# Two-layer MLP behind a retention: VectorE makes the low parts of the first MLP's weights, and the first block's queues stand in another order

## The chip, the cores and the metric

One core of a Trainium2 chip runs the whole program as one launch. The metric is the device time of that launch in microseconds, the median over several executions. TensorE multiplies, VectorE, ScalarE and GpSimd do the elementwise work, and SyncE issues every DMA. Each engine works through its own queue in the order in which the program was written (the kernel fixes its schedule by hand), and waits at the head of the queue until what the next instruction needs is there.

## The reference

The reference computes a retention over 4 sequences of 576 tokens with 8 heads of 64 dimensions, then two MLPs on the 2304 tokens of 512 features.

```
scores = q @ k.T / 8
ret    = scores * gamma_h ** (i - j)   for i >= j, else 0
x      = ret @ v                        # heads side by side: 2304 x 512
h  = relu(x @ w_in)                     # 512 -> 2048
x1 = (h * h) @ w_out                    # 2048 -> 512
h2  = x1 @ w2_in
out = (h2 * clip(h2 + 3, 0, 6) / 6) @ w2_out
```

All inputs and outputs are float32.

## The kernel before

Tokens come in chunks of 128, and blocks of chunks: the first MLP goes over blocks of 512, 384, 512, 384 and 512 tokens, then the second MLP over five blocks. The 2048 hidden features are 16 slices of 128, called `f`. One step is one slice in one block: `h_part` multiplies the block's `x` by slice `f` of the first weight and makes `g`, and `a_part` multiplies `g` by slice `f` of the second weight into accumulators that stay in PSUM for the whole block.

Float32 products are made of three passes in a narrower float format. Each operand is split into a high part (the value rounded to that format) and a low part (the value less its high part), and a product is high times high, plus low weight times high, plus high weight times low. So each of `h_part` and `a_part` is 12 matmuls of up to 512 columns: four pieces of 128 by three terms.

The weights arrive as 64-bit words and are taken apart in the first block, while the matmuls of that block already run. For slice `f`, half 0 is the first weight and half 1 the second:

- `load_w` issues the DMA for each half (512 KB each).
- `scale_w` (lines 128 and 129) is two ScalarE operations on the raw words.
- `narrow_w` (lines 144 and 145) is two VectorE operations that make the float32 value `wt`.
- `split_w` makes the high part `w[:, 0]` by a copy, on ScalarE (line 156), or for half 1 from slice 2 on VectorE (line 154, a cast), and the low part `w[:, 1]` by a subtraction (line 158): on GpSimd for the first MLP's weights, on VectorE for the second's, whose weights are taken apart in the same buffers while the last block of the first MLP runs.

For one step `h_part` ends with ScalarE's relu (line 459), VectorE's product `r` (460), ScalarE's copy of it to the high part of `g` (466, in the first block; in later blocks VectorE does it, 468) and VectorE's subtraction for the low part (469).

The retention of the first block's four chunks stands ahead of all this (`first_scores`, `first_values`, `first_x` and so on). `first_sum` makes the running state, four small VectorE operations for each chunk. The chunks of the next block, three of them for the second, are worked on between the steps of the block before, one piece in each step: `scale_k` and `age_state` on GpSimd, `scores` on TensorE with its followers on VectorE (`p` at line 366 or 370, state at 381 or 383) and `scale_q` on GpSimd, `values` on TensorE with `x` on ScalarE and VectorE (429, 430), and `load_chunk` for a chunk further on.

The loop at line 624 goes over all steps and writes, for step `f` of the first block, in this order: narrow half 1 of slice `f+1`, split half 0 of `f+2`, split half 1 of `f+1`; `h_part` of step `f+1`; the loads; the retention's piece; narrow half 0 of `f+3`; the scales of half 1 of `f+2` and half 0 of `f+4`; `a_part` of step `f`. Two accumulators' worth of PSUM for `h` and two buffers of `g` let TensorE run about one step ahead of VectorE's `g`.

Of the kernel before, what the change touches and what calls it, by code (L numbers as in the profile page):

```python
# [9 lines left out]
F32 = mybir.dt.float32  # L10
# [5 lines left out]
ALU = mybir.AluOpType  # L16
# [7 lines left out]
NC = DM // P  # L24
NF = DFF // P
# [56 lines left out]
def retention_moe_kernel(ctx: ExitStack, tc, qk, kv, w1, w2, cst, out):  # L82
# [5 lines left out]
    nc = tc.nc  # L88
# [24 lines left out]
    def load_w(ph, f, halves=(0, 1)):  # L113

        src = (w1, w2)[ph].bitcast(I32)
        for i in halves:
            t = wpool.tile([P, DM, 2], I32, tag=f"w{f}_{i}", name=f"raw_{ph}_{f}_{i}")
            nc.sync.dma_start(
                t, src[f, :, 2 * DM * i : 2 * DM * (i + 1)].rearrange("p (n t) -> p n t", t=2)
            )  # L120
            raws[ph, f, i] = t

    def scale_w(ph, f, halves=(0, 1)):
        for i in halves:
            raw = raws[ph, f, i]
            low, high = raw[:, :, 0], raw[:, :, 1]
            high = high.bitcast(F32)
            nc.scalar.activation(high, high, AF.Prelu, scale=2.0**-112, alpha=-(2.0**32))  # L128
            nc.scalar.activation(low, low.bitcast(U32), AF.Copy, scale=2.0**-29)  # L129
# [18 lines left out]
    def split_w(ph, f, halves=(0, 1), on_dve=False):  # L148

        for i in halves:  # L150
            t = wts[ph, f, i]
            w = wpool.tile([P, 2, DM], F32R, tag=f"w{f}_{i}", name=f"w_{ph}_{f}_{i}")
            if on_dve:
                nc.vector.tensor_copy(w[:, 0, :], t)
            else:
                nc.scalar.activation(w[:, 0, :], t, AF.Copy)  # L156
            eng = nc.vector if ph else nc.gpsimd
            eng.tensor_tensor(w[:, 1, :], t, w[:, 0, :].bitcast(F32), ALU.subtract)  # L158
            wts[ph, f, i] = w


# [8 lines left out]
    n0 = BLOCKS[0][0][0] // P  # L170
# [3 lines left out]
    def load_chunk(c):  # L174
        if c >= NCHUNK:
            return
        if 2 <= c < n0:
            t = wpool.tile([P, 2, NPAIR, P], F32, tag=f"w{NF - 2}_{c % 2}", name=f"q_{c}")
            kv_t = wpool.tile([P, 2, DM], F32, tag=f"w{NF - 3}_{c % 2}", name=f"kv_{c}")
        else:  # L180
            t = rawp.tile([P, 2, NPAIR, P], F32, tag="q", name=f"q_{c}")
            kv_t = rawp.tile([P, 2, DM], F32, tag="kv", name=f"kv_{c}")
        q, kt = t[:, 0], t[:, 1]
        if c == 0:
            nc.sync.dma_start(q, qk[c, :, 0, :].rearrange("p (n t) -> p n t", n=NPAIR))
            nc.sync.dma_start(con[:, QD0:DK0], cst[:, QD0:DK0])
            nc.sync.dma_start(kt, qk[c, :, 1, :].rearrange("p (n t) -> p n t", n=NPAIR))
            nc.sync.dma_start(con[:, :QD0], cst[:, :QD0])
            nc.sync.dma_start(kv_t[:, 1], kv[c, :, 1])
        else:  # L190
            nc.sync.dma_start(t, qk[c].rearrange("p x (n t) -> p x n t", n=NPAIR))
        if 2 <= c < n0:
            nc.sync.dma_start(kv_t, kv[c])
        elif c >= n0:

            for g in range(2):
                nc.sync.dma_start(
                    kv_t[64 * g : 64 * g + 64].rearrange("t x (r e) -> t x r e", r=2),
                    kv[c, :, :, 4 * D * g : 4 * D * (g + 1)].rearrange("(r t) x e -> t x r e", r=2),
                )  # L200
        ch[c] = q, kt, kv_t[:, 0, :], kv_t[:, 1, :]
        if c == 1:
            nc.sync.dma_start(ch[0][2], kv[0, :, 0])
            nc.sync.dma_start(kv_t, kv[1])
# [87 lines left out]
    def first_sum(c):  # L292
        st = sts.pop(c)
        for e in range(2):
            r = slice(64 * e, 64 * e + 64)
            s0, s = (state[i % 2][r, :, 64 * e : 64 * e + 64] for i in (c, c + 1))
            g = gc[r].unsqueeze(2).to_broadcast([64, NPAIR, 64])
            if c == 0:
                nc.vector.tensor_tensor(s, st[r], g, ALU.mult)
            else:  # L300
                nc.vector.tensor_tensor(s, st[r], s0, ALU.add)
                nc.vector.tensor_tensor(s, s, g, ALU.mult)
# [135 lines left out]
    def h_part(ph, blk, f):  # L438
        nb = BLOCKS[ph][blk][0]
        w = wts[ph, f, 0]  # L440
        x = xs[ph, blk]
        hp = ps_h.tile([P, 512], F32, tag="h", name=f"h_{ph}_{blk}_{f}")
        order = [(c, wi, xi) for wi, xi in ((0, 0), (1, 0), (0, 1)) for c in range(NC)]

        parts = 2 if ph == blk == f == 0 else 1
        for i in range(parts):
            ts = slice(i * nb // parts, (i + 1) * nb // parts)
            for k, (c, wi, xi) in enumerate(order):
                nc.tensor.matmul(  # L449
                    hp[:, ts],  # L450
                    w[:, wi, c * P : (c + 1) * P],
                    x[:, xi, c, ts],
                    start=k == 0,
                    stop=k == 3 * NC - 1,
                )
        r = tmpp.tile([P, 512], F32, tag="tmp", name=f"r_{ph}_{blk}_{f}")
        r = r[:, :nb]
        if ph == 0:
            nc.scalar.activation(r, hp[:, :nb], AF.Relu)  # L459
            nc.vector.tensor_tensor(r, r, hp[:, :nb], ALU.mult)  # L460
        else:
            nc.scalar.activation(r, hp[:, :nb], AF.Relu, bias=con3)  # L462
            nc.vector.scalar_tensor_tensor(r, r, 6.0, hp[:, :nb], ALU.min, ALU.mult)  # L463
        g = gpool.tile([P, 2, 512], F32R, tag="g", name=f"g_{ph}_{blk}_{f}")
        if ph == 0 and blk == 0:
            nc.scalar.activation(g[:, 0, :nb], r, AF.Copy)  # L466
        else:
            nc.vector.tensor_copy(g[:, 0, :nb], r)  # L468
        nc.vector.tensor_tensor(g[:, 1, :nb], r, g[:, 0, :nb].bitcast(F32), ALU.subtract)  # L469
        gts[ph, blk, f] = g  # L470
# [138 lines left out]
    split_w(0, 0, (1,))  # L609
    first_states(3)  # L610
    h_part(0, 0, 0)
    scale_w(0, 1, (1,))
    load_chunk(n0)
    load_chunk(n0 + 1)
    narrow_w(0, 2, (0,))
    split_w(0, 2, (0,))

# [6 lines left out]
    for i, (ph, blk, f) in enumerate(steps):  # L624
        if ph == 0 and blk == 0 and f + 1 < NF:
            narrow_w(0, f + 1, (1,))
            if 2 < f + 2 < NF:
                split_w(0, f + 2, (0,))
            split_w(0, f + 1, (1,), on_dve=f > 0)
            if f == 0:  # L630
                first_sum(n0 - 1)
        if i + 1 < len(steps):
            h_part(*steps[i + 1])
        if ph == 0:
            if blk == 0:
                if f + 4 < NF:
                    load_w(0, f + 4)
            if blk + 1 < nblk:
                n = BLOCKS[0][blk + 1][0] // P

                j, slot = divmod(f - 1, 5) if blk == 0 else divmod(f, 4)
                if f == 0:
                    new_x(0, blk + 1)
                if 0 <= j < n:
                    c = start[0][blk + 1] // P + j
                    if slot == 0:
                        scale_k(c)
                        age_state(c)
                    elif slot == 1:
                        scores(c)  # L650
                        scale_q(c)
                    elif slot == (3 if blk == 0 else 2):
                        values(c, xs[0, blk + 1], j * P)
                    elif slot == (4 if blk == 0 else 3):
                        load_chunk(c + 2)
            elif f == 0:
                attn_stack.close()
                pool2 = ctx.enter_context(tc.tile_pool(name="pool2", bufs=1))
        if ph == 0 and blk == 0:
            if f == 0:  # L660
                scale_w(0, 3, (0,))
            if f + 3 < NF:
                narrow_w(0, f + 3, (0,))
            for n, j in ((f + 2, 1), (f + 4, 0)):
                if n < NF:
                    scale_w(0, n, (j,))
        for stage, fn in enumerate((split_w, narrow_w, scale_w)):
            for n in todo.get(i - (nblk - 1) * NF + stage, ()):
                fn(1, n // 2, (n % 2,))
        a_part(ph, blk, f)  # L670
        if ph == 0 and blk == nblk - 1:
            load_w(1, f)
            if 8 <= f < 8 + NC:
                load_x1(0, f - 8)
        if ph == 1 and blk + 1 < nblk and 8 <= f < 8 + NC:
            load_x1(blk + 1, f - 8)
# [37 lines left out]
```

## Time and profile before

| | us |
|---|---|
| median of 3 runs | 875.55 |
| lowest and highest | 874.52, 876.18 |
| the profiled execution's own time | 876.04 |
| its span in the profile | 874.3 |
| TensorE busy (matmuls) | 860.0 |
| VectorE busy | 458.5 |
| ScalarE busy | 227.8 |
| GpSimd busy | 95.9 |

Times of single instructions below are from the profiled execution, counted from the start of its span. The granted TensorE clock was 1.00 of full speed over the whole span. The profile lists for each instruction its start and its duration, and in brackets the idle time of its engine just before it with the engine, tile and line that ended this idle time. PE is TensorE, DVE VectorE, ACT ScalarE, POOL GpSimd. Busy times of an engine can overlap by some hundredths of a microsecond, since an operation may start before the one ahead of it has written its last element.

### The profile page before, as it was taken

Reading aid. Unit: us, or ns where it says so; the run is one execution under the profiler, and the core shown is the slowest. Engines: PE = TensorE matmul, PEld = TensorE weight load, DVE = VectorE, ACT = ScalarE, POOL = GpSimd, SP = SyncE. Lnnn points to the kernel's source line nnn. Section 1 sums busy time; section 2 is a strip of 40 time slices with the busy share of each in tenths; the row PEclk is TensorE's granted clock in tenths of the full one; section 3 lists DMA queues with packets and bytes.
Section 4 is the critical chain, followed back from the end, with each engine's and each line's share of the span. In section 5 each row is a group of like instructions: output and inputs, shape, how many; then the busy total and the mean of one; then the engine's idle time right before and its main releaser. Section 6 shows DMA issues by size and latency. Waiting matters only on the chain.

```text
span 874.3 us, 12831 instructions
## 1 busy us (share of the span) xinstructions
PE 860.0 (98%) x5356; PEld 741.5 (85%) x5356; DVE 458.5 (52%) x778; ACT 227.8 (26%) x394; POOL 95.9 (11%) x86
## 2 busy tenths in 40 slices
PE   8899999999999999999999999999999999999998
PEld 7677779999888899998888998888888888888996
DVE  6788875445444355445788785335333533344333
ACT  2666641111111111114555642111111111111111
POOL 3455560101111011000000000000000000000000
PEclk9999999999999999999999999999999999999999
DMA  9956212112111021016565300100010001001001
GB/s 340 315 203 236 97 49 98 49 49 85 49 49 46 3 96 50 2 38 206 199 213 175 97 13 13 61 1 13 28 57 1 13 35 41 1 10 47 2 1 37
DMA packets 29130, 68.15 MB, mean 78 GB/s; under 512 B 2832, under 2 KB 12176, under 8 KB 29072
## 3 DMA queue, kind: packets, MB, share of 16 engines
q1 hardware_dynamic: 29072, 67.33, 23.2%
q8 instruction: 42, 0.69, 0.3%
q14 instruction: 16, 0.13, 0.1%
HBM read 57.88 MB, written 9.44 MB: 77 GB/s over the span
## 4 chain that ended last, share of the span: by engine, by line
PE 86%; DMA 5%; DVE 3%; issue 2%; POOL 1%; ACT 1%; SPq 0%; POOLq 0%; DVEq 0%; ACTq 0%
PE h L449 41%; PE acc L493 23%; PE acc L491 19%; DMA raw<-w_dram 3%; DMA q<-qk_dram 2%; PE o L420 1%; PE o L410 1%; PE sc L338 1%; POOL w L158 1%; DVE wt L145 1%; DVE wt L144 1%; DVE r L460 0%; PE sc L353 0%; ACT g L466 0%; POOL q L309 0%
## 5 line engine op out<-in xcount | busy, mean ns | idle before, releaser
L449 PE MATMUL h<-x,w 128*128 128x512 f32 (+2 forms) x1932 | 423.4, 367 | 5.8 <-ACT w L156 3.7
L449 PEld LDWEIGHTS h<-x,w 128*128 128x128 f32 x1932 | 351.4, 188 | 56.6 <-ACT w L156 5.7
L491 PE MATMUL acc<-g,w 128*128 128x512 f32 (+1 forms) x960 | 213.7, 371 | 1.0 <-ACT g L466 1.0
L493 PE MATMUL acc<-w,g 128*128 128x512 f32 x864 | 210.2, 391 | 0.3 <-DVE ev L514 0.3
L491 PEld LDWEIGHTS acc<-g,w 128*128 128x128 f32 x960 | 173.5, 188 | 24.3 <-ACT g L466 1.4
L493 PEld LDWEIGHTS acc<-w,g 128*128 128x128 f32 x864 | 161.5, 188 | 33.2 <-DVE ev L514 0.8
L463 DVE SCALAR_TENSOR_TENSOR r<-r,h 128x512 f32<-128x512 f32 (+1 forms) x80 | 50.7, 634 | 203.1 <-ACT r L462 203.0
L462 ACT ACTIVATE r<-h,con 128x512 f32<-128x512 f32 (+1 forms) x80 | 51.7, 646 | 311.3 <-PE h L449 305.8
L460 DVE TENSOR_TENSOR r<-r,h 128x512 f32<-128x512 f32 (+1 forms) x80 | 50.6, 632 | 148.9 <-ACT r L459 148.8
L469 DVE TENSOR_TENSOR g<-r,g 128x512 fp32r<-128x512 f32 (+1 forms) x160 | 108.2, 676 | 16.2 <-ACT g L466 11.2
L459 ACT ACTIVATE r<-h 128x512 f32<-128x512 f32 (+1 forms) x80 | 44.2, 552 | 240.6 <-PE h L449 233.7
L468 DVE CAST g<-r 128x512 fp32r<-128x512 f32 (+1 forms) x144 | 65.1, 452 | 14.6 <-DVE r L460 0.5
L145 DVE CUSTOM_DVE_ANT_0 wt<-raw,wt 128x1024 uint16<-128x1024 uint16 x64 | 47.1, 737 | 4.5 <-DVE wt L144 0.6
L158 POOL TENSOR_TENSOR w<-wt,w 128x512 fp32r<-128x512 f32 x32 | 42.7, 1339 | 53.0 <-ACT w L156 43.9
L128 ACT ACTIVATE raw<-raw 128x512 f32<-128x512 f32 x64 | 42.8, 669 | 2.6 <-DMA raw<-w_dram 2.6
L129 ACT ACTIVATE raw<-raw 128x512 int32<-128x512 uint32 x64 | 42.8, 669 | 0.0
L309 POOL TENSOR_TENSOR q<-q,con 128x512 f32<-128x512 f32 x13 | 18.2, 1402 | 175.7 <-issue 115.7
L156 ACT ACTIVATE w<-wt 128x512 fp32r<-128x512 f32 x50 | 30.8, 627 | 13.3 <-DVE wt L145 13.1
L144 DVE TENSOR_SCALAR wt<-raw 128x512 int32<-128x512 int32 x64 | 30.3, 474 | 0.1
L158 DVE TENSOR_TENSOR w<-wt,w 128x512 fp32r<-128x512 f32 x32 | 21.3, 685 | 0.0
L466 ACT ACTIVATE g<-r 128x512 fp32r<-128x512 f32 x16 | 10.1, 633 | 29.9 <-DVE r L460 29.9
L514 DVE TENSOR_SCALAR ev<-acc 128x512 f32<-128x512 f32 (+1 forms) x18 | 11.8, 658 | 9.1 <-DMA x<-ev 4.1
(47 smaller groups left out, 273.1 us busy)
## 6 DMA issues: line engine op xcount, KB each, us to landing
raw<-w_dram SPq DMA_DIRECT2D x64, 512.0 KB, 5.8
q<-qk_dram SPq DMA_DIRECT2D x17, 512.0 KB, 3.7
kv<-kv_dram SPq DMA_DIRECT2D x30, 256.0 KB, 4.9
out_dram<-ev SPq DMA_DIRECT2D x18, 256.0 KB, 2.1
x<-ev SPq DMA_DIRECT2D x12, 256.0 KB, 2.1
x1r<-x SPq DMA_DIRECT2D x12, 256.0 KB, 4.6
kv<-kv_dram SPq DMA_DIRECT2D x3, 512.0 KB, 7.9
x<-ev SPq DMA_DIRECT2D x8, 192.0 KB, 1.9
```

The source lines that it names most:

```text
L128: nc.scalar.activation(high, high, AF.Prelu, scale=2.0**-112, alpha=-(2.0**32))
L145: nc.vector.tensor_tensor(ti, ti, low, ALU.add)
L158: eng.tensor_tensor(w[:, 1, :], t, w[:, 0, :].bitcast(F32), ALU.subtract)
L449: nc.tensor.matmul(hp[:, ts], w[:, wi, c * P : (c + 1) * P], x[:, xi, c, ts], start=k == 0, stop=k == 3 * NC - 1,)
L459: nc.scalar.activation(r, hp[:, :nb], AF.Relu)
L460: nc.vector.tensor_tensor(r, r, hp[:, :nb], ALU.mult)
L462: nc.scalar.activation(r, hp[:, :nb], AF.Relu, bias=con3)
L463: nc.vector.scalar_tensor_tensor(r, r, 6.0, hp[:, :nb], ALU.min, ALU.mult)
L468: nc.vector.tensor_copy(g[:, 0, :nb], r)
L469: nc.vector.tensor_tensor(g[:, 1, :nb], r, g[:, 0, :nb].bitcast(F32), ALU.subtract)
L491: nc.tensor.matmul(acc[d][:, :nb], wt[:, sl], gt, start=first, stop=stop)
L493: nc.tensor.matmul(acc[d], gt[:, sl], wt, start=first, stop=stop)
```

## The change

The low part of the first MLP's weights is made by VectorE like that of the second's, for all 32 halves. In the first block `h_part` takes its terms in another order, so that the low part of the weight comes last. Slice 4 is loaded ahead of chunk 4, chunk 5 is loaded two steps later, `first_sum` of the last chunk stands behind step 1's `h_part`, the scale of slice 4's half 0 comes one step later, and from step 1 on half 0 of slice `f+3` is narrowed ahead of the retention's piece. The line numbers of the changed kernel are one lower from line 158 on up to `h_part`, and one higher behind the new `terms` line.

```diff
@@ split_w
-            eng = nc.vector if ph else nc.gpsimd
-            eng.tensor_tensor(w[:, 1, :], t, w[:, 0, :].bitcast(F32), ALU.subtract)
+            nc.vector.tensor_tensor(w[:, 1, :], t, w[:, 0, :].bitcast(F32), ALU.subtract)
@@ h_part
-        order = [(c, wi, xi) for wi, xi in ((0, 0), (1, 0), (0, 1)) for c in range(NC)]
+
+        terms = ((0, 0), (0, 1), (1, 0)) if ph == blk == 0 else ((0, 0), (1, 0), (0, 1))
+        order = [(c, wi, xi) for wi, xi in terms for c in range(NC)]
@@ ahead of the loop
     scale_w(0, 1, (1,))
+    load_w(0, 4)
     load_chunk(n0)
-    load_chunk(n0 + 1)
     narrow_w(0, 2, (0,))
@@ in the loop
             split_w(0, f + 1, (1,), on_dve=f > 0)
-            if f == 0:
-                first_sum(n0 - 1)
         if i + 1 < len(steps):
             h_part(*steps[i + 1])
         if ph == 0:
             if blk == 0:
-                if f + 4 < NF:
+                if f == 0:
+                    first_sum(n0 - 1)
+                elif f == 1:
+                    scale_w(0, 4, (0,))
+                if f + 3 < NF and f > 0:
+                    narrow_w(0, f + 3, (0,))
+                if 0 < f < NF - 4:
                     load_w(0, f + 4)
+                if f == 2:
+                    load_chunk(n0 + 1)
@@ behind the retention's piece
                 scale_w(0, 3, (0,))
-            if f + 3 < NF:
-                narrow_w(0, f + 3, (0,))
+                narrow_w(0, 3, (0,))
             for n, j in ((f + 2, 1), (f + 4, 0)):
-                if n < NF:
+                if n < NF and (n, j) != (4, 0):
                     scale_w(0, n, (j,))
```

In the rows of the order below, `wt_10_0` is slice 10's half 0, `w_9_1` slice 9's half 1 after the split, `r_0_8` is `r` of step 8 in the first block (0), `p` and `state` belong to the retention; the last number of a name only counts tiles.

VectorE, the beginning of the first block, from the first narrowed weight to `r` of step 0, before:

```order
L144 TENSOR_SCALAR wt_0_0_286<-raw_0_0_135 128x512
L145 ISA wt_0_0_286<-raw_0_0_135,wt_0_0_286 128x1024
L269 TENSOR_TENSOR x_0_152<-o_259,x_0_152 128x4x128
L269 TENSOR_TENSOR x_0_152<-o_296,x_0_152 128x2x128 x2
L144 TENSOR_SCALAR wt_1_0_317<-raw_1_0_137 128x512
L145 ISA wt_1_0_317<-raw_1_0_137,wt_1_0_317 128x1024
L144 TENSOR_SCALAR wt_0_1_323<-raw_0_1_139 128x512
L145 ISA wt_0_1_323<-raw_0_1_139,wt_0_1_323 128x1024
L460 TENSOR_TENSOR r_0_0_362<-r_0_0_362,h_0_0_337 128x512
```

VectorE, the same place in the changed kernel:

```order
L144 TENSOR_SCALAR wt_0_0_286<-raw_0_0_135 128x512
L145 ISA wt_0_0_286<-raw_0_0_135,wt_0_0_286 128x1024
L157 TENSOR_TENSOR w_0_0_292<-wt_0_0_286,w_0_0_292 128x512
L268 TENSOR_TENSOR x_0_152<-o_259,x_0_152 128x4x128
L268 TENSOR_TENSOR x_0_152<-o_296,x_0_152 128x2x128 x2
L144 TENSOR_SCALAR wt_1_0_317<-raw_1_0_137 128x512
L145 ISA wt_1_0_317<-raw_1_0_137,wt_1_0_317 128x1024
L157 TENSOR_TENSOR w_1_0_320<-wt_1_0_317,w_1_0_320 128x512
L144 TENSOR_SCALAR wt_0_1_323<-raw_0_1_139 128x512
L145 ISA wt_0_1_323<-raw_0_1_139,wt_0_1_323 128x1024
L157 TENSOR_TENSOR w_0_1_326<-wt_0_1_323,w_0_1_326 128x512
L461 TENSOR_TENSOR r_0_0_362<-r_0_0_362,h_0_0_337 128x512
```

Behind each narrowed weight there now stands a subtraction that reads ScalarE's copy of that same weight, and each is ahead of everything that VectorE does later.

VectorE, from `r` of step 8 to `r` of step 9, with chunk 5's scores between, before:

```order
L460 TENSOR_TENSOR r_0_8_834<-r_0_8_834,h_0_8_821 128x512
L469 TENSOR_TENSOR g_0_8_837<-r_0_8_834,g_0_8_837 128x512
L370 TENSOR_TENSOR p_877<-sc_844,con 128x768
L383 TENSOR_TENSOR state_93<-sc_844,state_93 64x4x64 x2
L144 TENSOR_SCALAR wt_10_0_882<-raw_10_0_786 128x512
L145 ISA wt_10_0_882<-raw_10_0_786,wt_10_0_882 128x1024
L144 TENSOR_SCALAR wt_9_1_901<-raw_9_1_732 128x512
L145 ISA wt_9_1_901<-raw_9_1_732,wt_9_1_901 128x1024
L154 CAST w_9_1_907<-wt_9_1_901 128x512
L460 TENSOR_TENSOR r_0_9_923<-r_0_9_923,h_0_9_910 128x512
```

VectorE, the same step in the changed kernel:

```order
L461 TENSOR_TENSOR r_0_8_834<-r_0_8_834,h_0_8_821 128x512
L470 TENSOR_TENSOR g_0_8_837<-r_0_8_834,g_0_8_837 128x512
L144 TENSOR_SCALAR wt_10_0_840<-raw_10_0_789 128x512
L145 ISA wt_10_0_840<-raw_10_0_789,wt_10_0_840 128x1024
L369 TENSOR_TENSOR p_880<-sc_847,con 128x768
L382 TENSOR_TENSOR state_93<-sc_847,state_93 64x4x64 x2
L144 TENSOR_SCALAR wt_9_1_901<-raw_9_1_735 128x512
L145 ISA wt_9_1_901<-raw_9_1_735,wt_9_1_901 128x1024
L157 TENSOR_TENSOR w_10_0_904<-wt_10_0_840,w_10_0_904 128x512
L154 CAST w_9_1_907<-wt_9_1_901 128x512
L157 TENSOR_TENSOR w_9_1_907<-wt_9_1_901,w_9_1_907 128x512
L461 TENSOR_TENSOR r_0_9_923<-r_0_9_923,h_0_9_910 128x512
```

The narrowing of slice 10 moved ahead of the retention's two groups, and two subtractions came in, one on either side of the cast.

GpSimd, steps 7 and 8 (`kv` is `scale_k`, `state` is `age_state`, `q` is `scale_q`, of chunk 5), before:

```order
L315 TENSOR_TENSOR kv_376<-kv_376,con 128x512
L397 TENSOR_TENSOR state_93<-state_94,con 64x4x64 x2
L158 TENSOR_TENSOR w_9_0_815<-wt_9_0_793,w_9_0_815 128x512
L158 TENSOR_TENSOR w_8_1_818<-wt_8_1_812,w_8_1_818 128x512
L309 TENSOR_TENSOR q_375<-q_375,con 128x512
L158 TENSOR_TENSOR w_10_0_904<-wt_10_0_882,w_10_0_904 128x512
```

GpSimd in the changed kernel, its operations for chunks 4, 5 and 6:

```order
L314 TENSOR_TENSOR kv_375<-kv_375,con 128x512
L308 TENSOR_TENSOR q_374<-q_374,con 128x512
L314 TENSOR_TENSOR kv_526<-kv_526,con 128x512
L396 TENSOR_TENSOR state_93<-state_94,con 64x4x64 x2
L308 TENSOR_TENSOR q_525<-q_525,con 128x512
L314 TENSOR_TENSOR kv_738<-kv_738,con 128x512
L396 TENSOR_TENSOR state_94<-state_93,con 64x4x64 x2
L308 TENSOR_TENSOR q_737<-q_737,con 128x512
```

No subtraction is left on GpSimd, so the operations of one chunk follow those of the chunk before directly in its queue.

## Rows read from the trace of the kernel before

**Rows 1.** Busy time by stretches of the span: start and end in us, their length, then for TensorE's matmuls, its weight loads, VectorE, ScalarE and GpSimd the busy us with the number of instructions, the granted clock, the DMA share and GB/s.

```profile
60.00:70.00 10.00, 10.00 (x45) 8.26 (x45) 8.22 (x13) 6.32 (x13) 5.20 (x4) 1.00 0.89 284
...
600.00:800.00 200.00, 200.00 (x884) 165.58 (x884) 78.86 (x135) 27.92 (x41) 0.00 (x0) 1.00 0.06 20
```

**Rows 2.** Waits of TensorE's matmuls over the whole span: the waiting line, what it waited for, then us in total, times, longest.

```profile
PE h L449 <- ACT w L156: 3.7, 3, 1.8
PE h L449 <- POOL w L158: 1.8, 5, 0.5
```

**Rows 3.** The timeline of TensorE's matmuls in the first block: start us, us, engine, line, operation, tiles, count, and idle time before with its releaser.

```profile
36.88 3.01 PE L491 MATMUL acc<-g,w 128*128 128x512 f32 x12 [0.99 <-ACT g L466]
41.74 1.20 PE L449 MATMUL h<-x,w 128*128 128x512 f32 x4 [1.85 <-ACT w L156]
...
65.48 2.88 PE L491 MATMUL acc<-g,w 128*128 128x512 f32 x12
68.20 2.88 PE L449 MATMUL h<-x,w 128*128 128x512 f32 x12
...
119.88 1.19 PE L449 MATMUL h<-x,w 128*128 128x512 f32 x4 [0.92 <-ACT w L156]
121.46 2.11 PE L449 MATMUL h<-x,w 128*128 128x512 f32 x8 [0.39 <-POOL w L158]
...
128.07 2.27 PE L449 MATMUL h<-x,w 128*128 128x384 f32 x12
```

**Rows 4.** VectorE's timeline over one step of the first block without a piece of the retention.

```profile
68.59 0.68 DVE L460 TENSOR_TENSOR r<-r,h 128x512 f32<-128x512 f32 x1
69.97 0.69 DVE L469 TENSOR_TENSOR g<-r,g 128x512 fp32r<-128x512 f32 x1 [0.70 <-ACT g L466]
70.58 0.42 DVE L144 TENSOR_SCALAR wt<-raw 128x512 int32<-128x512 int32 x1
71.03 0.69 DVE L145 CUSTOM_DVE_ANT_0 wt<-raw,wt 128x1024 uint16<-128x1024 uint16 x1
71.64 0.42 DVE L144 TENSOR_SCALAR wt<-raw 128x512 int32<-128x512 int32 x1
72.20 0.69 DVE L145 CUSTOM_DVE_ANT_0 wt<-raw,wt 128x1024 uint16<-128x1024 uint16 x1
72.92 1.42 DVE L154 CAST w<-wt 128x512 fp32r<-128x512 f32 x1
74.27 0.68 DVE L460 TENSOR_TENSOR r<-r,h 128x512 f32<-128x512 f32 x1
```

**Rows 5.** VectorE's timeline in the last block of the first MLP, where it makes the low parts of the second's weights and GpSimd does nothing.

```profile
416.81 0.69 DVE L158 TENSOR_TENSOR w<-wt,w 128x512 fp32r<-128x512 f32 x1
417.41 0.42 DVE L144 TENSOR_SCALAR wt<-raw 128x512 int32<-128x512 int32 x1
...
421.18 0.43 DVE L468 CAST g<-r 128x512 fp32r<-128x512 f32 x1
421.64 0.69 DVE L469 TENSOR_TENSOR g<-r,g 128x512 fp32r<-128x512 f32 x1
```

**Rows 6.** The timeline of VectorE and ScalarE: the first narrowed weight, the copy of `w_0_0`, and `r` of steps 1 and 4.

```profile
21.60 0.43 DVE L144 TENSOR_SCALAR wt<-raw 128x512 int32<-128x512 int32 x1
...
22.89 0.63 ACT L156 ACTIVATE w<-wt 128x512 fp32r<-128x512 f32 x1 [0.28 <-DVE wt L145]
...
35.48 0.69 DVE L460 TENSOR_TENSOR r<-r,h 128x512 f32<-128x512 f32 x1
...
56.60 0.69 DVE L460 TENSOR_TENSOR r<-r,h 128x512 f32<-128x512 f32 x1
```

**Rows 7.** VectorE's timeline: one operation of `first_sum` with GpSimd idle, and the two groups behind chunk 5's scores.

```profile
20.25 0.42 DVE L302 TENSOR_TENSOR state<-state,con 64x256 f32<-64x256 f32 x1
...
83.61 0.95 DVE L370 TENSOR_TENSOR p<-sc,con 128x768 f32<-128x768 f32 x1
84.48 0.87 DVE L383 TENSOR_TENSOR state<-sc,state 64x256 f32<-64x256 f32 x2
```

**Rows 8.** ScalarE's timeline: the scale of slice 4's half 0.

```profile
39.95 0.67 ACT L128 ACTIVATE raw<-raw 128x512 f32<-128x512 f32 x1 [0.87 <-DMA raw<-w_dram]
40.52 0.65 ACT L129 ACTIVATE raw<-raw 128x512 int32<-128x512 uint32 x1
```

**Rows 9.** The timelines of GpSimd and VectorE in the third block, where `scale_q` and `scale_k` follow each other.

```profile
222.01 1.28 POOL L309 TENSOR_TENSOR q<-q,con 128x512 f32<-128x512 f32 x1 [14.77 <-issue]
223.25 1.23 POOL L315 TENSOR_TENSOR kv<-kv,con 128x512 f32<-128x512 f32 x1
...
222.52 1.05 DVE L468 CAST g<-r 128x512 fp32r<-128x512 f32 x1
223.61 1.42 DVE L469 TENSOR_TENSOR g<-r,g 128x512 fp32r<-128x512 f32 x1
```

**Rows 10.** The timelines of GpSimd and VectorE in step 7 of the first block, where `scale_k` and `age_state` run.

```profile
75.68 1.56 POOL L315 TENSOR_TENSOR kv<-kv,con 128x512 f32<-128x512 f32 x1
76.25 1.27 DVE L144 TENSOR_SCALAR wt<-raw 128x512 int32<-128x512 int32 x1
...
77.55 0.98 DVE L145 CUSTOM_DVE_ANT_0 wt<-raw,wt 128x1024 uint16<-128x1024 uint16 x1
...
78.46 0.84 DVE L144 TENSOR_SCALAR wt<-raw 128x512 int32<-128x512 int32 x1
```

## Prediction

> **What bounds the kernel now.** I read the busy time by stretches first: from 600 to 800 us TensorE is busy for 200.00 of 200 us [rows 1]. So nothing after the first token block can gain or lose from this change, and a delay of the first block goes to the end undiminished. Nearly all of TensorE's waits are for the weights of `h` (line 449), high part from ScalarE or low part from GpSimd [rows 2]. TensorE's timeline shows where they lie: before `a_1` (36.88), before `h_3` (41.74) and before `h_15` (119.88, with a second gap ahead of the eight matmuls that begin with the low part, 121.46) [rows 3]. The third of the three waits for ScalarE [rows 2] is one like it five steps earlier, at `h_10`. The first block ends for TensorE when `h` of the second block starts, at 128.07 [rows 3].
>
> What lies behind these waits is VectorE's queue. From the `r` of one step (line 460) to that of the next, 68.59 to 74.27, VectorE pauses once only, 0.70 us between `r` and `g` for ScalarE's copy; everything else is back to back [rows 4]. That plain step takes 5.68 us, while TensorE needs 12 + 12 matmuls, twice the 2.72 from 65.48 to 68.20 [rows 3], so 5.44. With the retention's share VectorE is a little slower than TensorE, and every five steps TensorE has used up its lead and waits. So **VectorE's order of work sets the first block**, and the question is what the change does to its queue.
>
> **The plain step.** Removed: the cast at line 154 took 1.42 us at 72.92, with GpSimd at a subtraction beside it [rows 4]; a cast of this size takes 0.43 where GpSimd is idle [rows 5]. Its cost in the step, from its start to the next `r`, is 1.35. Added: two subtractions. VectorE runs them in the second layer in 0.69, the next operation 0.60 behind the start [rows 5]. An operation that reads a cast comes 0.46 behind it (421.18 to 421.64) [rows 5]. New step: `r` to `g` 1.38, then 0.61, 0.45, 0.61, 0.56 as now up to the second line 145, then 0.61 for it, 0.61 + 0.46 + 0.61 for subtraction, cast, subtraction: **5.90 us against 5.68**. Two subtractions come in and GpSimd's disturbance of the cast goes out, and they nearly cancel.
>
> **The opening.** The first chain starts at 21.60 in both kernels. ScalarE's copy of `w_0_0` runs 22.89 to 23.52 [rows 6]. VectorE now stands waiting for it (it went on with `x` before), subtracts at 23.55, does the three `x` operations (1.3), narrows `w_1_0` from 25.5 to 26.7, waits 0.63 for its copy, subtracts, narrows `w_0_1`, waits for the copy, subtracts at 29.75, and reaches `r_0` at 30.4. `g_0` follows 1.38 later, then two more such rounds (narrow 1.1, wait 0.65, subtract 0.61) for `w_2_0` and `w_1_1`: `r_1` at 37.4 instead of 35.48 [rows 6]. In these five rounds the new queue puts a round trip through ScalarE where GpSimd used to take the subtraction off VectorE's hands. Putting the matmuls on the low part last hides the subtraction itself from TensorE, but not this.
>
> Then by steps of 5.90. `r_2`: plus the four operations of `first_sum`, moved behind `g_1`, 0.42 each (20.25) [rows 7] and 1.8 with what lies between: 37.4 + 5.90 + 1.8 = 45.1. `r_3` and `r_4`: plus chunk 4's two groups on VectorE, taken like chunk 5's, 0.87 + 0.87 (83.61, 84.48) [rows 7], and one wait: ScalarE now does six scale operations, 0.57 from one to the next (39.95, 40.52) [rows 8], between the copy of `g_2` and that of `w_4_0`, so the copy ends 0.54 + 3.4 + 0.63 = 4.6 after the former began, and VectorE wants it 0.68 + 0.61 + 1.06 + 1.17 = 3.5 after: 1.1. `r_4` at 45.1 + 11.8 + 1.74 + 1.1 = 59.7, instead of 56.60 [rows 6]. Order of loads: `w_4_0` is no longer late (ScalarE stood for its transfer until 39.95 [rows 8], which made the wait of `h_3`). That gain is real for TensorE, but VectorE, 3 us behind, takes its place as the last to come. Chunk 4 comes behind 1 MB of weights; at the 284 GB/s of 60 to 70 us [rows 1] that is 3.7 us, and its scores are wanted only behind `h_3`. I cost that at nothing.
>
> **Steps 4 to 14.** Ten steps of 5.90, two `x` of 0.60 (as one such operation follows another [rows 5]) and two chunks of 1.74 [rows 7]: 63.7, so `r_14` at 123.4, if GpSimd disturbs nothing. Narrowing ahead of the retention removes the late copy that ScalarE waits for at `h_10` and `h_15`; what is late next is the subtraction of the low part, in the same VectorE queue.
>
> **GpSimd's rest.** Its four operations for each chunk stay. With the subtractions gone they start as soon as the scores are through, `scale_q` of one chunk and `scale_k` of the next together. The nearest rows are in the third block, where GpSimd already runs that pair (222.01, 223.25): the cast beside it takes 1.05 and the subtraction 1.42 [rows 9], against 0.43 and 0.69 alone [rows 5], so 1.35 are lost. Three such pairs fall before `r_14`: 4.05. `age_state` comes twice: in the pair of `scale_k` and `age_state` at 75.68 VectorE's operations at 76.25, 77.55 and 78.46 took 1.27, 0.98, 0.84 [rows 10] against 0.42, 0.69, 0.42 [rows 4], together 1.56, of which 0.71 are the second's. I take half of that for each, 0.7 in all, since some fall on VectorE's pause. Together 4.75; bounds 0 (all fall on pauses or on operations that read PSUM) and 9.0 (three pairs of 1.28 + 1.23 [rows 9] in full, and 0.71 twice).
>
> What the rows show is that VectorE's operations stretch until GpSimd's end, subtractions with two inputs in SBUF too (223.61) [rows 9]. The Trainium skill, page "SBUF — State Buffer", section "Who interferes with whom", says the shared port pair is an exclusive lock and that whoever comes second "fully blocks"; it counts VectorE instructions with two SBUF inputs among those blocked. The trace agrees for 1.42 against 0.69. Taken to the letter for every pair it gives the upper bound, and it speaks against this change, since all 32 added operations are of that kind and GpSimd's own become freer to start.
>
> **The end of the block.** `r_14` at 123.4 + 4.75 = 128.15. The low part of `w_15_0` starts 0.61 + 0.46 + 0.61 ahead of it and takes 0.69: ready at 127.2. Before, it was ready at 121.46, and from there to 128.07 TensorE took 6.61 [rows 3], with eight matmuls of `h_15` still to do. Now four are left, which saves 4 x 0.227 = 0.9 (twelve matmuls take 2.72): 127.2 + 5.7 = 132.9, or **4.8 us later**. The profiled execution took 876.04; 880.85 by its measure, and it lay 0.5 above the median of 875.55, so 880.4.
>
> **Rivals.** (1) No lock: GpSimd's operations cost VectorE nothing. Then the block ends at 128.15, and the time is 875.6 to 876: no difference. For it speaks that at 75.68 GpSimd's 1.56 are themselves a stretched operation, so VectorE sometimes wins; against it, that VectorE has one pause of 0.7 in 5.9 us. (2) Faster: TensorE, not VectorE, sets the pace. If VectorE's order leaves enough lead, the gaps ahead of `a_1`, `h_3`, `h_10` and `h_15` go: 0.99 + 1.85 + two times 1.6 (0.92 idle at 119.88, then 0.67 between four matmuls of 0.227 and 121.46) [rows 3], about 6 us, so 869.5, or some 872 when the opening keeps part of its wait. For it: VectorE is busy only 8.22 of 10 us [rows 1]; a step would have to take under 5.4 us, though, and the pause between `r` and `g` holds nothing new in the new order. (3) Full lock: every GpSimd operation takes its whole time from VectorE, 9.0 instead of 4.75: 884.6. The Trainium skill's page named above states this as the rule; the rows show it only where VectorE was in the way. It decides if the pairs always start in the middle of narrowing, which now stands ahead of the retention, just where the scores end.
>
> **How the numbers follow.** My forecast, 877.4 to 883, gets 0.66; no difference 0.16; faster 0.10; full lock 0.08. The likeliest is 880.4. The range runs from 875.0, which takes in the first rival, to 884.5, just short of the third. A measurement of this kernel can tell about 0.2% from no change: slower by more than that (over 877.3) 0.74, within 0.16, faster 0.10.
>
> **What the new profile would show.** Right: `r` to `r` 5.9 us in plain steps on VectorE with only the pause for `g`; line 154 at about 0.43; `r_1` near 37.4 and `r_14` near 128; TensorE waiting on VectorE's low part or on `g` in most steps; `h` of the second block at about 133; nothing changed from there on. Wrong: a plain step below 5.5, or TensorE without gaps between 60 and 120; then rival 2 holds. If VectorE's steps with scores take as little as 7.6, rival 1.

## The result, and the profile after

The changed kernel takes **886.11 us** (median of 4 runs, 884.43 to 886.91), the kernel before 875.04 (4 runs, 874.52 to 876.18): a ratio of 1.012, 95% interval 1.0107 to 1.0132. It is slower, as forecast, but by 11.1 us instead of 4.8, and outside the range. The profiled execution took 885.89 with a span of 884.1, 9.8 more than the span before; the medians lie 11.1 apart because the profiled execution of before was 1.0 above its median and this one 0.2 below.

TensorE's timeline of the changed kernel, the places that answer to [rows 3] and what follows them:

```profile
38.28 3.02 PE L492 MATMUL acc<-g,w 128*128 128x512 f32 x12 [1.28 <-ACT g L467]
42.63 3.03 PE L450 MATMUL h<-x,w 128*128 128x512 f32 x12 [1.33 <-ACT w L156]
...
128.51 1.20 PE L450 MATMUL h<-x,w 128*128 128x512 f32 x4 [0.49 <-DVE w L157]
131.38 3.00 PE L492 MATMUL acc<-g,w 128*128 128x512 f32 x12
136.27 3.33 PE L450 MATMUL h<-x,w 128*128 128x384 f32 x12 [1.89 <-ACT x L428]
139.39 3.58 PE L492 MATMUL acc<-g,w 128*128 128x512 f32 x12
142.81 2.27 PE L450 MATMUL h<-x,w 128*128 128x384 f32 x12
```

`a_1` starts 1.40 later than before, `h_3` 0.89 later, the low-weight part of `h_15` (now four matmuls, 128.51) well behind. `a_14` starts at 131.38, in the trace of before at 125.24: 6.1 later. Then comes something that the prediction did not have: TensorE stands 1.89 us for an `x`, and `h` of the second block starts at 136.27 instead of 128.07 [rows 3], 8.2 later. It and the `a_15` behind it run longer than their like (3.33 against 2.27, 3.58 against 3.00), and the next `h` is at 142.81, before at 132.94: 9.9 later. That is the whole difference of the spans (9.8).

Busy time by stretches of the changed kernel, columns as in [rows 1]:

```profile
134.00:136.00 2.00, 0.38 (x2) 0.00 (x0) 1.30 (x3) 0.90 (x2) 0.00 (x0) 1.00 1.04 311
136.00:138.00 2.00, 1.73 (x8) 1.73 (x9) 1.06 (x2) 0.21 (x1) 0.00 (x0) 0.84 0.22 43
138.00:140.00 2.00, 2.00 (x7) 1.91 (x7) 0.00 (x0) 0.37 (x1) 0.00 (x0) 0.50 0.00 0
140.00:142.00 2.00, 2.00 (x9) 1.60 (x8) 1.47 (x3) 0.45 (x2) 0.00 (x0) 0.81 0.00 0
142.00:144.00 2.00, 2.00 (x12) 1.83 (x11) 0.69 (x1) 0.87 (x2) 0.00 (x0) 1.00 0.41 153
...
600.00:860.00 260.00, 260.00 (x1179) 219.32 (x1178) 102.67 (x181) 37.46 (x57) 0.00 (x0) 1.00 0.06 21
```

The longer matmuls have their reason in the granted clock: behind the gap it falls to 0.50 (the 1.2 GHz level) and is back at 1.00 by 142. Before, it was 1.00 throughout. Not every execution of the changed kernel has this fall: the mean clock of the span was 0.998 in three of them (885.89 to 886.91 us) and 1.000 in the fourth, which was the fastest (884.43). From 600 on TensorE is full, as in [rows 1].

The `x` that TensorE waits for is chunk 6's, the last of the second block. VectorE's and ScalarE's timelines at the end of the first block of the changed kernel, from `r_14` on:

```profile
129.55 0.69 DVE L461 TENSOR_TENSOR r<-r,h 128x512 f32<-128x512 f32 x1
...
134.39 0.68 DVE L461 TENSOR_TENSOR r<-r,h 128x512 f32<-128x512 f32 x1
135.76 0.69 DVE L470 TENSOR_TENSOR g<-r,g 128x512 fp32r<-128x512 f32 x1 [0.69 <-ACT g L467]
136.37 0.68 DVE L429 TENSOR_TENSOR x<-o,x 128x512 fp32r<-128x512 f32 x1
...
135.10 0.63 ACT L467 ACTIVATE g<-r 128x512 fp32r<-128x512 f32 x1 [2.59 <-DVE r L461]
135.64 0.58 ACT L428 ACTIVATE x<-o 128x512 fp32r<-128x512 f32 x1
```

Both of its operations stand behind `g` of step 15, on ScalarE and on VectorE. So this `x` inherits the whole delay of VectorE's queue, although its matmuls were done before `a_14`. The matmuls of `h` begin as soon as ScalarE's part is there (135.64 + 0.58 against 136.27). The same two operations in the kernel before:

```profile
126.63 0.58 ACT L429 ACTIVATE x<-o 128x512 fp32r<-128x512 f32 x1
...
127.36 0.68 DVE L430 TENSOR_TENSOR x<-o,x 128x512 fp32r<-128x512 f32 x1
```

There ScalarE's part was done at 127.21, 0.86 ahead of `h` at 128.07 [rows 3].

VectorE's timeline of the changed kernel over a plain step, as [rows 4], and over the next one, in which GpSimd runs `scale_q` and `scale_k` (its two rows below):

```profile
73.65 0.68 DVE L461 TENSOR_TENSOR r<-r,h 128x512 f32<-128x512 f32 x1
75.02 0.69 DVE L470 TENSOR_TENSOR g<-r,g 128x512 fp32r<-128x512 f32 x1 [0.70 <-ACT g L467]
...
77.86 0.69 DVE L157 TENSOR_TENSOR w<-wt,w 128x512 fp32r<-128x512 f32 x1
78.47 0.42 DVE L154 CAST w<-wt 128x512 fp32r<-128x512 f32 x1
78.92 0.69 DVE L157 TENSOR_TENSOR w<-wt,w 128x512 fp32r<-128x512 f32 x1
79.53 0.68 DVE L461 TENSOR_TENSOR r<-r,h 128x512 f32<-128x512 f32 x1
...
81.97 1.69 DVE L145 CUSTOM_DVE_ANT_0 wt<-raw,wt 128x1024 uint16<-128x1024 uint16 x1
83.59 1.26 DVE L144 TENSOR_SCALAR wt<-raw 128x512 int32<-128x512 int32 x1
...
87.26 0.68 DVE L461 TENSOR_TENSOR r<-r,h 128x512 f32<-128x512 f32 x1
...
81.82 1.30 POOL L308 TENSOR_TENSOR q<-q,con 128x512 f32<-128x512 f32 x1 [17.95 <-issue]
83.07 1.50 POOL L314 TENSOR_TENSOR kv<-kv,con 128x512 f32<-128x512 f32 x1
```

The plain step takes 79.53 - 73.65 = 5.88, the step with the pair 87.26 - 79.53 = 7.73: the pair costs 1.85.

TensorE's waits over the whole span, as [rows 2]:

```profile
PE acc L492 <- ACT g L467: 5.6, 9, 1.3
PE h L450 <- ACT w L156: 3.1, 4, 1.3
...
PE h L450 <- DVE w L157: 1.2, 3, 0.5
```

The waits for GpSimd's low part are gone. In their place TensorE now waits mostly for `g`, in nine steps: VectorE is late everywhere, not only where a weight is.

### The profile page after: what moved, and what is told of

The parts are those of the page before. It is cut to its first block, busy times and chain, and to the rows that moved or that the text cites. A ratio compares the mean times of both kernels' runs of the same rounds, so it can differ in the third digit from the quotient of the medians.

```text
span 884.1 us, 12781 instructions
## 1 busy us (share of the span) xinstructions
PE 862.9 (98%) x5356; PEld 741.0 (84%) x5356; DVE 467.8 (53%) x810; ACT 227.5 (26%) x394; POOL 51.5 (6%) x54
## 4 chain that ended last, share of the span: by engine, by line
PE 84%; DVE 9%; issue 3%; ACT 3%; DMA 1%; POOL 0%; SPq 0%; DVEq 0%; ACTq 0%; POOLq 0%
PE h L450 40%; PE acc L494 22%; PE acc L492 18%; DVE wt L145 2%; DVE wt L144 2%; DVE w L157 1%; PE o L419 1%; DVE r L461 1%; PE o L409 1%; ACT g L467 1%; PE sc L337 1%; DVE g L470 1%; DMA kv<-kv_dram 1%; ACT w L156 1%; DVE w L154 0%
## 5 line engine op out<-in xcount | busy, mean ns | idle before, releaser
L470 DVE TENSOR_TENSOR g<-r,g 128x512 fp32r<-128x512 f32 (+1 forms) x160 | 108.5, 678 | 16.1 <-ACT g L467 11.1
L157 DVE TENSOR_TENSOR w<-wt,w 128x512 fp32r<-128x512 f32 x64 | 43.4, 687 | 4.2 <-ACT w L156 3.7
L396 POOL TENSOR_TENSOR state<-state,con 64x256 f32<-64x256 f32 x18 | 13.2, 735 | 71.2 <-PE o L419 45.1
```

What stands on the lines that cost most here:

```text
L157: nc.vector.tensor_tensor(w[:, 1, :], t, w[:, 0, :].bitcast(F32), ALU.subtract)
```

## The experiments

In the expectations, theory A is the one of the prediction: the slowdown is VectorE's queue with the 32 subtractions in it. The other letters stand for what each expectation says of them. After the result A had two additions, the wait for chunk 6's `x` and the clock behind it. Ratios are to the kernel before, run on the same chip (875.15, 875.35 and 875.3 us).

**The subtractions alone.** The kernel before, with the engine changed and nothing else:

```diff
-            eng = nc.vector if ph else nc.gpsimd
+            eng = nc.vector
```

> The kernel before, with the low parts of the first MLP's weights made by VectorE and nothing else changed. Theory A (the 32 subtractions in VectorE's queue cost the time, the new order does not): as slow as the changed kernel or some 2 us slower, 886 to 889, since the copies of h_10 and h_15 stay behind the retention and the low part is still wanted after four matmuls. Rival B (the new order costs it: narrowing ahead of the retention meets GpSimd's pair, and the loads stand differently): 875 to 878.

886.07 us (885.42 to 886.29), ratio 1.0124 (1.0109 to 1.014): all of the slowdown. TensorE's timeline of this kernel at `a_1` and at `h` of the second block:

```profile
41.07 4.61 PE L491 MATMUL acc<-g,w 128*128 128x512 f32 x12 [3.47 <-ACT g L466]
...
137.40 2.35 PE L449 MATMUL h<-x,w 128*128 128x384 f32 x12 [1.05 <-ACT x L429]
```

Here the opening waits longest: 3.47, and the 12 matmuls behind take 4.61 instead of 3.02, at a clock of 0.50. The new order saves 2.8 us of this at `a_1` and 1.1 at the second block's `h`; in the changed kernel the fall of the clock at the block's end takes that back.

**The new order alone.** The changed kernel with the subtraction back where it was:

```diff
-            nc.vector.tensor_tensor(w[:, 1, :], t, w[:, 0, :].bitcast(F32), ALU.subtract)
+            eng = nc.vector if ph else nc.gpsimd
+            eng.tensor_tensor(w[:, 1, :], t, w[:, 0, :].bitcast(F32), ALU.subtract)
```

> The changed kernel with the first MLP's low parts back on GpSimd: the new order alone. Theory A: somewhat faster than before, 871 to 874, since the waits ahead of a_1 and h_3 (1.0 and 1.85 us) go and narrowing comes ahead of the retention; r_1 at about 33.6 us. Rival B: 880 or more.

875.74 us (10 runs), ratio 1.0005 (0.9996 to 1.0015): no difference. The order does no harm; that it would gain 1 to 4 us was wrong. VectorE's plain step is 5.68 here too (68.00 to 73.68, the cast 1.43), and other waits came (GpSimd's `scale_k` 2.4 in three places).

**Chunk 6's `x` ahead of `g_15`.** The changed kernel, with the followers of `h_15` written behind those of the values of chunk 6 (`h_post` is the rest of `h_part`, from `r` on):

```diff
         if i + 1 < len(steps):
-            h_part(*steps[i + 1])
+            late = h_part(*steps[i + 1], defer=i == NF - 2)
...
                         load_chunk(c + 2)
+                if i == NF - 2:
+                    late()
```

> The changed kernel, with relu, r and g of step 15 written behind the x of chunk 6 instead of ahead of it; TensorE's order is the same. Theory A (h of the second block waits 1.9 us for an x that stands behind g_15, and the clock falls for some us behind that gap): h of the second block at about 134.2 us instead of 136.27, clock at full speed from 136 to 142, 882.4, 3.7 us less than the changed kernel. Rival C (TensorE would wait there for something else, r_15 or g_15, and the clock falls all the same): less than 1 us gained, 885 to 886.

883.16 us (882.75 to 884.77), ratio 1.0096 (1.0081 to 1.0111): 2.95 less than the changed kernel. TensorE's timeline:

```profile
134.34 2.27 PE L450 MATMUL h<-x,w 128*128 128x384 f32 x12
...
139.64 2.27 PE L450 MATMUL h<-x,w 128*128 128x384 f32 x12
```

No wait, `h` 1.93 earlier, the `h` after it 3.17 earlier, and the granted clock 1.00 in every two microseconds from 128 to 144. So the wait and the clock together are worth 3 of the 11 us; 3.7 were expected.

**The gap filled.** The changed kernel, with idle matmuls ahead of `h` of the second block; the wait stays, only TensorE isn't idle in it:

```diff
+        if i == NF - 1:
+            idle_matmuls(7)
         if i + 1 < len(steps):
```

> The changed kernel with seven matmuls of 128 columns on zeros, read by nobody, ahead of h of the second block, where TensorE stood idle for 1.9 us. Theory A (the idle time itself makes the clock fall): the wait stays, the clock stays at full speed from 136 to 142 us, the twelve matmuls of h take 2.1 instead of 3.1 us and those of a_15 2.8 instead of 3.4: 884.4, 1.7 us less than the changed kernel. Rival C (the clock falls for the many smaller gaps before): no change, 886.

885.41 us (884.9 to 886.9), ratio 1.0123 (1.0106 to 1.014). The intervals overlap those of the changed kernel, so the time alone decides nothing. TensorE's timeline:

```profile
132.00 3.03 PE L492 MATMUL acc<-g,w 128*128 128x512 f32 x12
134.87 1.72 PE L547 MATMUL unread<-nought 128*128 128x128 f32 x14
136.89 2.35 PE L450 MATMUL h<-x,w 128*128 128x384 f32 x12 [0.30 <-ACT x L428]
...
141.85 2.27 PE L450 MATMUL h<-x,w 128*128 128x384 f32 x12
```

The granted clock is 1.00 in every two microseconds from 120 to 144. From `a_14` to the second `h` it takes 141.85 - 132.00 = 9.85 instead of 142.81 - 131.38 = 11.43: 1.6 less, which is the clock's price in the profiles. That the fill is what kept the clock is not shown: in two of the runs below it stayed at 1.00 behind a gap there that was as long or longer and that nothing filled. This execution was 0.63 later from `r_1` on (37.51 against 36.88), far ahead of the fill, so that only 0.96 is left at the second `h`.

**Without GpSimd's work.** The changed kernel without `scale_q`, `scale_k` and `age_state` in the first block (that part of the retention is left out):

```diff
-                        scale_k(c)
-                        age_state(c)
+                        if blk:
+                            scale_k(c)
+                            age_state(c)
...
-                        scale_q(c)
+                        if blk:
+                            scale_q(c)
```

> The changed kernel without GpSimd's scale_q, scale_k and age_state for chunks 4 to 6 (left out, so these chunks' retention isn't the reference's). Theory A (of the queue's growth, GpSimd's pairs take 1.9 us each and age_state 0.7, read from the steps of the changed kernel, 7.73 and 6.61 against 5.88): r_14 at about 122.5 instead of 129.55, every step without retention 5.88, 879, 7 us less than the changed kernel. Rival D (GpSimd's rest falls on time that VectorE has to spare): 884 or more.

880.46 us (879.44 to 882.08), ratio 1.0061 (1.0046 to 1.0076): 5.65 less than the changed kernel. `r_14` starts at 123.83 (129.55 with that work), the plain step is 5.88 as before. Some 7 were expected; the next section says where the rest went. The wait for `x` and the low clock stay:

```profile
130.55 3.91 PE L450 MATMUL h<-x,w 128*128 128x384 f32 x12 [1.87 <-ACT x L428]
```

**The opening on GpSimd.** The changed kernel, where the first five low parts are GpSimd's again (in this and the next edits the subtraction is then issued on `eng`):

```diff
+            eng = nc.vector if ph or f > 2 or (f, i) == (2, 1) else nc.gpsimd
```

> The changed kernel with the first five low parts (slices 0 and 1, and half 0 of slice 2) back on GpSimd. Theory A (each of these five rounds makes VectorE wait 0.7 us for ScalarE's copy and subtract for 0.6): r_1 at about 33.5 instead of 36.88, and since VectorE sets the pace all the way, 2.8 to 3.4 us carried to the end: 883. Rival E (the opening is hidden, TensorE waits for the weights' transfers there anyway): 885.5 or more.

881.99 us (881.4 to 883.34), ratio 1.008 (1.0063 to 1.0097): 4.1 less. `r_1` is at 33.66 instead of 36.88, `r_14` at 127.17 instead of 129.55: of 3.2 us in the opening 2.4 reach the end. The rest is the clock: TensorE stands 1.89 for the same `x`, yet in this profile the clock stays at 1.00 behind it (2.4 + 1.7 = 4.1). It fell in the opening instead, behind a wait of 2.21 for a weight's copy ahead of `h_3`, here from 42 to 44:

```profile
42.00:44.00 2.00, 2.00 (x6) 1.55 (x6) 1.51 (x3) 0.39 (x1) 0.00 (x0) 0.55 1.05 292
```

From `r_1` to `r_2` this kernel gave back 0.9 of its lead (42.89 against 45.19).

**Only half 0 on VectorE.** The changed kernel, where VectorE makes the low parts of half 0 from slice 3 on and GpSimd those of half 1:

```diff
+            eng = nc.vector if ph or (i == 0 and f > 2) else nc.gpsimd
```

> The changed kernel with VectorE making the low parts of half 0 from slice 3 on alone, and GpSimd all the others. Theory A (VectorE's queue is the bound, and it was the subtraction of half 0 on GpSimd that stretched VectorE's cast, 1.42 against 0.43, while the one of half 1 runs beside r and the pause): a plain step of 1.38 + 0.61 + 0.45 + 0.61 + 0.56 + 0.61 + 0.61 + 0.35 = 5.2, below TensorE's 5.44, so TensorE sets the pace between the retention's pieces: 868 to 872, faster than both kernels. Rival F (GpSimd's remaining subtraction stretches another operation of VectorE's instead): 874 to 877.

871.58 us (871.25 to 872.11), ratio 0.9958 (0.9944 to 0.9973): **faster than both**. The plain step is 5.16, under the 5.44 that TensorE needs. With chunk 6's `x` ahead as well:

> As the run with half 0 alone, and the x of chunk 6 ahead of relu, r and g of step 15. Theory A: h of the second block waits for x a little there too; 0 to 1 us less than that run. Rival C: no difference.

870.58 us (870.31 to 872.41), ratio 0.9951 (0.9936 to 0.9966): the same within the intervals, since there is no wait for that `x` any more.

**Only half 1 on VectorE.** Its mirror, with one subtraction more on VectorE in all:

```diff
+            eng = nc.vector if ph or (i == 1 and f > 1) else nc.gpsimd
```

> The mirror of the run in which VectorE made half 0's low parts: the changed kernel, where VectorE makes the low parts of half 1 only (from slice 2 on) and GpSimd those of half 0. The same number of subtractions on VectorE as in that run (14 against 13). Theory A (which subtraction stays on GpSimd decides): half 0's comes just ahead of half 1's cast and stretches it to 1.42 again, so the plain step is 5.68 + 0.61 = 6.2 to 6.3 us, TensorE waits in every step, h of the second block comes at 132 to 136, the time is 880 to 886. Theory D (only how many subtractions VectorE has decides): the plain step is 5.1 to 5.3 as in that run, and the time 870.5 to 873.

884.35 us (883.79 to 886.0), ratio 1.0105 (1.0089 to 1.0122): A, not D (`h` of the second block, at 136.42, is just past the 132 to 136 expected). VectorE's and GpSimd's timelines of this kernel:

```profile
69.11 1.40 DVE L154 CAST w<-wt 128x512 fp32r<-128x512 f32 x1
70.55 0.69 DVE L158 TENSOR_TENSOR w<-wt,w 128x512 fp32r<-128x512 f32 x1
71.15 0.68 DVE L462 TENSOR_TENSOR r<-r,h 128x512 f32<-128x512 f32 x1
...
68.84 1.38 POOL L158 TENSOR_TENSOR w<-wt,w 128x512 fp32r<-128x512 f32 x1 [5.59 <-ACT w L156]
```

Half 0's subtraction on GpSimd (68.84) runs beside half 1's cast, which takes 1.40 instead of 0.42; that step (`r` at 64.18 to `r` at 71.15), less 0.60 for an `x` in it, takes 6.4. So it counts which of the two a step gives to VectorE.

**Only half 0, in the old order.** The kernel before with that line alone:

```diff
-            eng = nc.vector if ph else nc.gpsimd
+            eng = nc.vector if ph or (i == 0 and f > 2) else nc.gpsimd
```

> The kernel before in its old order, where VectorE makes half 0's low parts from slice 3 on and GpSimd all others. Theory A (VectorE's plain step falls to about 5.2 us in this order too, and what is left are the waits that the old order of loads and of the retention makes: 1.85 ahead of h_3, and up to 1.6 ahead of h_10 and h_15 for the copy behind the retention): 872.5 to 875, so the new order is worth 1 to 3 us once VectorE's queue has slack. Theory E (with slack in VectorE's queue the order is worth nothing): 871 to 872. Theory F (the new order is what made the step short): plain step over 5.5, 875 to 880.

**869.67 us** (869.1 to 870.2), ratio 0.9934 (0.9919 to 0.9949): the fastest, below the 871.58 of the same line in the new order. None of the three theories had that: with slack in VectorE's queue the new order comes out 1.9 us slower. The four runs of each lie apart (869.1 to 870.2 against 871.25 to 872.11), though the intervals of the two ratios just overlap. VectorE's and GpSimd's timelines, then TensorE's:

```profile
59.63 0.42 DVE L154 CAST w<-wt 128x512 fp32r<-128x512 f32 x1
59.97 0.68 DVE L460 TENSOR_TENSOR r<-r,h 128x512 f32<-128x512 f32 x1
61.34 0.69 DVE L469 TENSOR_TENSOR g<-r,g 128x512 fp32r<-128x512 f32 x1 [0.70 <-ACT g L466]
...
60.18 1.30 POOL L158 TENSOR_TENSOR w<-wt,w 128x512 fp32r<-128x512 f32 x1 [3.98 <-DVE w L154]
```

```profile
41.05 3.01 PE L449 MATMUL h<-x,w 128*128 128x512 f32 x12 [0.86 <-ACT w L156]
...
122.26 2.27 PE L449 MATMUL h<-x,w 128*128 128x384 f32 x12
```

Half 1's subtraction follows the cast, so on GpSimd it falls under `r`, which reads `h` from PSUM and still takes 0.68, and under the pause ahead of `g`: 1.30 us that cost VectorE nothing. TensorE has no wait from 45.4 to the second block's `h` at 122.26, 5.8 earlier than [rows 3]. The waits ahead of `h_10` and `h_15` are gone though their order is the old one, and that of `h_3` is 0.86 instead of 1.85 [rows 3]: for the most part they had been VectorE's lateness.

What the new order costs here stands in the three steps with a chunk's scores: they take 6.83, 7.14 and 7.45 in the old order and 7.93, 8.23 and 8.56 in the new one, 1.1 more each. In the middle one of them, VectorE's and GpSimd's timelines in the old order, then in the new one:

```profile
79.69 0.94 DVE L370 TENSOR_TENSOR p<-sc,con 128x768 f32<-128x768 f32 x1
...
79.17 1.76 POOL L309 TENSOR_TENSOR q<-q,con 128x512 f32<-128x512 f32 x1
...
81.02 1.52 DVE L144 TENSOR_SCALAR wt<-raw 128x512 int32<-128x512 int32 x1
...
80.50 1.75 POOL L309 TENSOR_TENSOR q<-q,con 128x512 f32<-128x512 f32 x1
```

In the old order `scale_q` runs beside `p`, which reads the scores from PSUM and takes 0.94, no more than the 0.95 that it takes with GpSimd idle (90.31 in the changed kernel). In the new order the narrowing stands there, and it takes 1.52 instead of 0.42. So `r_14` comes at 118.53 instead of 115.37, and `h` of the second block at 124.08 instead of 122.26. By these rows it is the narrowing ahead of the retention that costs; no run moved it alone.

## Why the prediction missed

**What bounds the kernel, and the mechanism: right.** VectorE's queue sets the first block, the subtractions alone make the slowdown, and nothing changes from the second `h` of the second block on. One reading was too wide: of the 9.8 us of waits of TensorE in the trace of before, 5.5 are for the weights of `h` [rows 2], and the one ahead of `a_1` is for `g` [rows 3].

**The plain step: right.** 5.88 measured, 5.90 forecast, with the cast at 0.42.

**The opening: right within its size.** `r_1` at 36.88 (37.4 forecast), `r_2` at 45.19 (45.1). That both came so near is in part luck: the first chain began at 20.89, not 21.60, the terms from `r_0` on as written add up to 37.1, and from `r_1` to `r_2` there was an idle time of 0.55 that the sum did not have. `r_4` came at 60.56 (59.7); the first pair of `scale_q` and `scale_k` lies in that stretch, and the prediction counted it in a later term. The wait of 1.1 for the copy of `w_4_0` does not show, since that pair's stretch covers it.

**Steps 4 to 14 without GpSimd: right.** Forecast `r_14` at 123.4, measured 123.83 in the run without that work.

**GpSimd's rest: mis-sized.** I took 4.75 from a pair's 1.35 in the third block [rows 9]. The pair costs 1.85 here, because it meets two operations of VectorE back to back (two of narrowing, 1.69 and 1.26 instead of 0.69 and 0.42), and a step with `age_state` takes 6.61, 0.73 over the plain one, where I took 0.35. Three such pairs and two of these make 7.0; taking the work away moved `r_14` by 5.7. The rows of that run account for the rest: the wait for the copy of `w_4_0` comes back (the step to `r_3` takes 6.93 instead of 5.88), and GpSimd, idle, starts the next `scale_k` of its queue, one written for the second block, already at 101.03, which costs a step 0.62; `r_1` was 0.28 earlier. `r_14` came at 129.55 against the forecast's 128.15: 1.4 of the miss, 1.0 of it from this term by that run (5.7 against 4.75), 0.4 from the steps without it.

**The end of the block: this step failed.** It reckoned "127.2 + 5.7 = 132.9" from the low part of `w_15_0` and the matmuls behind it, as if `h` of the second block needed nothing else. It also needs chunk 6's `x`, whose two operations stand behind `g_15` in the queues that I had just made late. Before, ScalarE's part of that `x` was done 0.86 ahead of TensorE (127.21 against 128.07) and no row showed a wait. TensorE's lead over VectorE was spent, so the hidden dependence became the bound: 1.9 us, and the clock behind the gap 1.7 more. The three shares, 1.4 + 1.9 + 1.7 = 5.0, are the 9.8 of the spans less the 4.8 forecast. That the last two go when the `x` comes earlier was shown by a run. That the clock's fall has a price of its own shows in profiles with the wait and without the fall (1.6 less with the gap filled, as much with the opening on GpSimd) and in the changed kernel's one run at a mean clock of 1.000 (884.43); why it fell in the others is not shown.

**The rivals.** No lock (875.6 to 876) fell with the stretched pair. The full lock gave 884.6. Much of its price in VectorE's queue is real (7.0 of 9.0 by the steps, 5.7 by the run without that work), but the time went past it by another way, the `x` and the clock. TensorE as the pace (869.5) was a rival for this change with a right condition, "a step would have to take under 5.4 us": moving only half 0's subtraction meets it with 5.16, and the time was 869.67. The prediction let two subtractions in and the shorter cast nearly cancel (5.68 to 5.90). It did not see that one of the two subtractions buys all of the gain (the cast from 1.42 to 0.42, for 0.61 of work: 5.68 to 5.16), and the other only costs (5.16 to 5.88), as GpSimd would have done it under an operation that reads PSUM.

## What to carry to other kernels

When a queue becomes late, list every operand of the first instruction behind the stretch, not only the one that is waited for now: the one that was just in time is the next wait. When work moves from GpSimd to VectorE, move only the piece that stands beside VectorE operations which stretch, and leave on GpSimd the one that falls under a pause or a read of PSUM. When VectorE's operations change places, look at which of them then stand beside GpSimd's. Compare the step with what TensorE needs, here 5.44: a step of 5.16 instead of 5.68 went with 5.6 us of gain, one of 5.88, with the opening, GpSimd's pairs, the `x` and the clock on top, with 11 of loss.

## What was not expected of the hardware

- After a gap of 1.89 us in the changed kernel, and of 1.87 without GpSimd's work, the granted clock fell to 0.50; after 1.89 at the same place with the opening on GpSimd, and 2.24 with only half 1 on VectorE, it stayed at 1.00. The length of the gap alone does not decide it in these four profiles; what does stays open. It differs from run to run of the same kernel too, as the four runs of the changed kernel show.
- A GpSimd subtraction of 1.29 to 1.38 us stretches a VectorE cast from 0.42 to 1.40, and leaves `r`, with one input in PSUM, at 0.68. The Trainium skill, page "SBUF — State Buffer", section "Who interferes with whom", says that a VectorE instruction with at most one SBUF input outside the two-port modes does not contend with GpSimd, and counts casts among those that can: these rows agree.
